# Attention probabilities and output rows turned as fp32 pairs of bf16

## The chip, the cores and the metric

The kernel runs on one core of a Trainium2 chip. The core has a matrix engine (TensorE, PE below, with its weight loads apart), a vector engine (VectorE, DVE), a scalar engine (ScalarE, ACT), GpSimd (POOL), and SyncE (SP), which here only issues DMAs. The metric is the device time of one launch in microseconds, lower is better.

## The reference

Two parts follow each other. A chunked attention: 4 batches, 8 heads, 768 tokens, head size 64. Each chunk of 32 queries sees 8 memory rows and a window of its own chunk with 16 tokens to the left and 8 to the right, so 64 keys.

```python
scores = scale * np.matmul(q_c, k_full.transpose(0, 1, 3, 2))
scores = scores - np.max(scores, axis=-1, keepdims=True)
a = np.exp(scores)
a = a / (np.sum(a, axis=-1, keepdims=True) + 1e-09)
out[:, :, c_start:c_end] = np.matmul(a, v_full)
```

Then a mixture of experts over the 3072 tokens of width 512 that come out: a router with noise picks two of 8 experts for each token, and each expert is a ReLU layer of width 1024.

```python
noisy_logits = logits + noise_scale * noise
top2 = np.argpartition(-noisy_logits, 2, axis=1)[:, :2]
...
h = np.maximum(x[mask] @ w1[e], 0.0)
out[mask] += top2_w[mask, k, None] * (h @ w2[e])
```

## The kernel before

The first stage holds attention and routing, the second the experts. The first runs a loop of 12 steps (`NT`, L538), three for each batch. Step `i` works on two tiles of 128 tokens (`j` = 0, 1) for all 8 heads at once. `b` is the batch, `tp` the step within it.

A step's own work, with the tiles that the prediction names:

- `scores` (L394): PE multiplies queries with keys and memory keys into `ps_s` (two banks of PSUM, one buffer); DVE takes the maximum (L416) and subtracts it (L418) into `sc`.
- `exps` (L421): ACT takes the exponential of the 1024 numbers of each row (L423) into `pb`, in bf16. For each head the two token tiles stand behind one another: 64 numbers of tile 0, 64 of tile 1.
- `turn_p` (L427): for each head PE turns a 128 by 128 block of `pb` against the bf16 identity `identb` (L430), eight turns, and ACT copies the result out of PSUM into `pT` (L433). A block holds both token tiles of one head, so after the turn tile 0 has partitions 0 to 63 and tile 1 has 64 to 127.
- `values` (L436): PE sums the rows with `ones2` (L440), multiplies with the value rows `vb` in 64 small products (L447), DVE takes the reciprocal (L452) and multiplies it in, one instruction for each token tile (L455), into `xrow`.
- `turn_x` (L461): the output rows of the step before are turned in eight blocks (L465) and copied by ACT into `xT` (L467); `gate` (L470) multiplies them with the router's weights `wgn` (L477).
- `keep_x` (L481): the rows go to DRAM, from where the experts gather them.

Beside that each step prepares later ones: `mix` (L349, by POOL after the start) orders loaded rows, `copy_unit` turns them on PE (L366) and copies them into `kT`, `qT` or `vT` (L375, nearly all by ACT), `windows` (L377) turns values into the window rows of `vb` (L383) with a copy by DVE (L386), and `memory_rows` (L388) sends the memory values `mvn` into `vb` by DMA from SP. At the second and third step of a batch a part of the routing of the batch before runs on DVE (L219 to L317).

In this stage the order on PE, ACT, DVE and SP is the order in which the program is written (`manual_schedule`, L512). Turned tiles of all kinds share three PSUM buffers (`psT`). Before the loop, memory keys, memory values and router weights come in through `stage`; the memory values are cast on DVE (L138), the router's weights by L143.

In the second stage `mm1` (L672) and `mm2` (L687) run the experts on tiles of 128 tokens that share the same two experts; the rows come in by gathers of POOL (L638) and leave by scatters (L644).

Of the kernel before, what the change touches and what calls it, by code (L numbers as in the profile page):

```python
# [22 lines left out]
def kernel(  # L23
# [104 lines left out]
    make_identity(nc, identb)  # L128

# [7 lines left out]
    mvn = keep.tile([B * NM, Dm], BF16, name="mvn")  # L137
    nc.vector.tensor_copy(mvn.rearrange("m (c g d) -> m c g d", c=HP, g=2), mvs.rearrange("m (g c) d -> m c g d", g=2))  # L138
    wgs = stage[:, 2 * D + Dm:2 * D + Dm + KP * 2 * E].rearrange("p (k e) -> p k e", k=KP)
    nc.scalar.dma_start(out=wgs[:, :, 0:E], in_=moe_w_gate.rearrange("(kp p) e -> p kp e", p=128))  # L140
    nc.scalar.dma_start(out=wgs[:, :, E:2 * E], in_=moe_w_noise.rearrange("(kp p) e -> p kp e", p=128))
    wgn = const.tile([128, KP, 2 * E], BF16, name="wgn")
    nc.vector.tensor_copy(wgn, wgs)  # L143
# [233 lines left out]
    def windows(b, tp, half):  # L377
        p_v = psT.tile([128, 2, HP, 128], BF16, name="p_v", tag="ps_t")
        for i in range(2):
            c0 = (8 * tp + 2 * half + i) * CH  # L380
            for c in range(HP):
                for j in range(2):
                    nc.tensor.transpose(out=p_v[j * 64:j * 64 + 64, i, c, :],  # L383
                                        in_=vT[:, c, c0 + j * 128:c0 + j * 128 + 64],
                                        identity=identb, tile_position=(0, j * 64))
        nc.vector.tensor_copy(vb[b % 2][:, tp, 2 * half:2 * half + 2], p_v)  # L386

    def memory_rows(b, tp):  # L388
        for j in range(2):
            r0 = j * 64 + WIN  # L390
            nc.sync.dma_start(out=vb[b % 2][r0:r0 + NM, tp].rearrange("m r c w -> m r (c w)"),
                              in_=mvn[b * NM:(b + 1) * NM].unsqueeze(1).to_broadcast([NM, 4, Dm]))

    def scores(t):  # L394
        b, tp = divmod(t, TP)
        q_, k_ = qT[b % 2], kT[b % 2]
        ps_s = psS.tile([128, HP, 2, 2, KW], F32, name="ps_s")
        for j in range(2):
            tk = (2 * tp + j) * 128
            for c in range(HP):  # L400
                nc.tensor.matmul(out=ps_s[:, c, j, :, WIN:KW], lhsT=q_[:, c, tk:tk + 128],
                                 rhs=mkT[:, c, b], start=True, stop=True)
        for j in range(2):
            for c in range(HP):
                for r in range(4):
                    tr = (2 * tp + j) * 128 + r * CH
                    nc.tensor.matmul(out=ps_s[r * CH:(r + 1) * CH, c, j, :, 0:WIN], lhsT=q_[:, c, tr:tr + CH],  # L407
                                     rhs=k_[:, :, c, tr:tr + WIN], start=True, stop=True,
                                     tile_position=(0, r * CH))
        if tp == 0:  # L410
            nc.vector.memset(ps_s[0:CH, :, 0, :, 0:LC], NEG)
        if tp == TP - 1:
            nc.vector.memset(ps_s[128 - CH:128, :, 1, :, WIN - RC:WIN], NEG)
        s3 = ps_s.rearrange("p c j g w -> p (c j g) w")
# [6 lines left out]
    def exps(sc):  # L421
        pb = work.tile([128, H, 2, KW], BF16, name="pb")
        nc.scalar.activation(out=pb.rearrange("p (g c) j w -> p g (c j) w", g=2),  # L423
                             in_=sc.rearrange("p (n g) w -> p g n w", g=2), func=Act.Exp, scale=scale)
        return pb

    def turn_p(pb):  # L427
        p_p = psT.tile([128, H, 128], BF16, name="p_p", tag="ps_t")
        for x in range(H):
            nc.tensor.transpose(out=p_p[:, x, :], in_=pb[:, x].rearrange("p j w -> p (j w)"),  # L430
                                identity=identb)
        pT = work.tile([128, H, 128], BF16, name="pT")
        nc.scalar.copy(pT, p_p)  # L433
        return pT

    def values(t, pT, between=None):  # L436
        b, tp = divmod(t, TP)
        ps_g = psG.tile([128, H, 2], F32, name="ps_g", tag="ps_g")
        for x in range(H):
            nc.tensor.matmul(out=ps_g[:, x], lhsT=pT[:, x, :], rhs=ones2, start=True, stop=True)  # L440
        ps_o = psO.tile([128, 2, H, D], F32, name="ps_o")
        for x in range(H):
            g, c = divmod(x, HP)
            for r in range(4):
                for j in range(2):
                    rows = slice(j * 64, j * 64 + 64)
# [542 lines left out]
```

## Time and profile before

| | us |
|---|---|
| median of 3 runs | 368.08 (367.45 to 370.07) |
| the profiled execution | 364.76 |
| its span, first to last instruction | 363.1 |
| PE busy in the span | 293.6 |
| DVE busy | 178.5 |
| ACT busy | 145.5 |
| POOL busy | 131.7 |

The page gives for each engine the busy time, then the span in 40 slices with the busy share in tenths, then groups of instructions as: line, engine, operation, output and input, shapes, count, busy time and mean of one in ns, and behind the bar the time that the engine sat idle just before them and what ended it. Matmul durations include the way through the array, so that eight in a row take far less than eight times one. "PEld" are the weight loads, which can lie under matmuls. The clock of PE is given as a share of its full speed.

### The profile page before, as it was taken

What the parts mean: (1) busy time and instruction counts of PE and PEld (TensorE: products, weight loads), DVE (VectorE), ACT (ScalarE), POOL (GpSimd) and SP (SyncE); (2) the same over time, 40 slices, a digit from 0 to 9 for tenths busy, and PEclk for the clock granted to TensorE, in tenths of its full rate; (3) what the DMA queues carried; (4) which work ended last, traced back from release to release, by engine and by line L of the source; (5) the groups of instructions that cost most, each with busy time, mean ns of one, the idle gap of its engine ahead of it and who ended that gap; (6) DMA issues with size and microseconds to landing.
All of it is one profiled execution on the core that took longest, in us unless ns stands there. A gap on an engine that the chain in (4) does not pass through costs nothing.

```text
span 363.1 us, 8521 instructions
## 1 busy us (share of the span) xinstructions
PE 293.6 (81%) x3636; PEld 195.0 (54%) x3636; DVE 178.5 (49%) x408; ACT 145.5 (40%) x202; POOL 131.7 (36%) x173
## 2 busy tenths in 40 slices
PE   0577777767776634299999999999999999999990
PEld 0566666656665533185554446666446666555540
DVE  7855565898799787631123410695320134322230
ACT  1446778866853513024433134312244311343400
POOL 6297254554030022572651734063174023201132
PEclk9999798896988755589999999999999999999997
DMA  7999869994949520149799999962059992100012
GB/s 130 213 213 202 160 126 216 210 219 77 201 92 181 127 65 31 33 121 152 126 205 229 202 158 217 152 89 98 23 151 172 193 225 86 54 25 3 23 49 75
DMA packets 44156, 48.33 MB, mean 133 GB/s; under 512 B 19367, under 2 KB 33447, under 8 KB 44112
## 3 DMA queue, kind: packets, MB, share of 16 engines
q0 software_dynamic: 22672, 40.51, 58.8%
q1 hardware_dynamic: 17296, 7.08, 11.4%
q10 hardware_dynamic: 4144, 0.13, 0.8%
q8 instruction: 30, 0.49, 0.5%
q14 instruction: 14, 0.11, 0.1%
HBM read 64.88 MB, written 10.55 MB: 208 GB/s over the span
## 4 chain that ended last, share of the span: by engine, by line
PE 32%; issue 18%; POOL 5%; DVE 4%; DMA 3%; POOLq 1%
PE p_h L681 17%; PE p_y L690 13%; POOL out_dram L644 4%; DMA out_dram<-y,main_dst 1%; DMA xTt<-xt 1%; DMA xt<-xd,main_src 1%; DVE w_all L455 1%; POOL xt L638 1%; DVE oh_l L303 1%; POOL w_all L816 0%; PE p_list L315 0%; PE p_xt L658 0%; POOLq L984 0%; DVE cum L297 0%; PE p_x L465 0%
## 5 line engine op out<-in xcount | busy, mean ns | idle before, releaser
L681 PE MATMUL p_h<-xTt,w_all 128*128 128x256 bf16 (+3 forms) x672 | 101.7, 311 | 0.0
L690 PE MATMUL p_y<-w_all,h 128*128 128x512 bf16 x448 | 100.0, 379 | 0.0
L681 PEld LDWEIGHTS <-w_all 128*128 128x128 bf16 x672 | 65.1, 99 | 34.8 <-issue 0.2
L669 ACT ACTIVATE h<-p_h 128x512 bf16<-128x512 f32 (+1 forms) x79 | 43.5, 551 | 91.2 <-PE p_h L681 80.2
L690 PEld LDWEIGHTS <-h 128*128 128x128 bf16 x448 | 43.7, 98 | 50.0
L667 DVE TENSOR_SCALAR h<-p_h 128x512 bf16<-128x512 f32 (+1 forms) x47 | 29.6, 630 | 75.7 <-PE p_h L681 69.4
L644 POOL DMA_INDIRECT out_dram<-y,main_dst x28 | 31.0, 1108 | 93.8 <-DVE y L696 72.1
L350 POOL COPY w_all<-w_all 128x1024 bf16<-128x1024 bf16 x30 | 30.6, 1044 | 28.9 <-PE p_t L366 27.3
L696 DVE SCALAR_TENSOR_TENSOR y<-p_y,main_w,y 128x512 f32<-128x512 f32 x28 | 21.0, 750 | 39.0 <-PE p_y L690 38.4
L366 PE MATMUL p_t<-identb,w_all 128*128 128x128 bf16 x288 | 27.9, 262 | 11.6 <-DVE w_all L350 7.2
L638 POOL DMA_INDIRECT xt<-xd,main_src x28 | 27.2, 972 | 23.2 <-DMA xTt<-xt 10.4
L694 ACT ACTIVATE y<-p_y,main_w 128x512 f32<-128x512 f32 x28 | 19.3, 689 | 36.5 <-PE p_y L690 35.4
L366 PEld LDWEIGHTS <-w_all 128*128 128x128 bf16 x288 | 23.2, 120 | 13.2 <-DVE w_all L350 7.6
L375 ACT COPY kT<-p_t 64x1024 bf16<-64x1024 bf16 x21 | 21.2, 1008 | 13.6 <-DVE kT L375 10.7
L383 PE MATMUL p_v<-identb,w_all 128*64 128x128 bf16 x384 | 19.0, 256 | 4.8 <-ACT w_all L375 3.3
L308 POOL TENSOR_TENSOR vals<-ohp,facts 128x1008 bf16<-128x1008 bf16 (+2 forms) x5 | 6.6, 1310 | 40.4 <-DVE facts L276 40.4
L433 ACT COPY pT<-p_p 128x1024 bf16<-128x1024 bf16 x12 | 12.1, 1010 | 21.3 <-PE p_p L430 21.1
L383 PEld LDWEIGHTS <-w_all 128*64 128x64 bf16 x384 | 15.1, 132 | 8.2 <-ACT w_all L375 4.2
L455 DVE TENSOR_TENSOR w_all<-ps_o,rs 128x512 bf16<-128x512 f32 x24 | 15.5, 686 | 6.2 <-PE ps_o L447 5.7
L467 ACT COPY xT<-p_x 128x1024 bf16<-128x1024 bf16 x12 | 12.2, 1013 | 13.9 <-PE p_x L465 13.9
L386 DVE COPY w_all<-p_v 128x1024 bf16<-128x1024 bf16 x24 | 16.2, 684 | 2.6 <-PE p_v L383 2.6
L416 DVE TENSOR_REDUCE mx<-ps_s 128x16 f32<-128x1024 f32 x12 | 14.7, 1224 | 4.6 <-PE ps_s L407 4.3
(177 smaller groups left out, 289.6 us busy)
## 6 DMA issues: line engine op xcount, KB each, us to landing
w_all<-in_moe_w_dram POOLq DMA_DIRECT2D x16, 1024.0 KB, 14.2
w_all<-in_moe_w_dram POOLq DMA_DIRECT2D x8, 512.0 KB, 13.9
w_all<-in_k_dram POOLq DMA_DIRECT2D x4, 768.0 KB, 10.4
w_all<-in_q_dram POOLq DMA_DIRECT2D x4, 768.0 KB, 9.6
w_all<-in_v_dram POOLq DMA_DIRECT2D x4, 768.0 KB, 12.1
xd<-w_all SPq DMA_DIRECT2D x12, 256.0 KB
w_all<-mvn SPq DMA_DIRECT2D x24, 32.0 KB
xt<-xd,main_src POOLq DMA_INDIRECT x28, 3.3
```

The source lines that it names most:

```text
L350: i = eng.tensor_copy(home(n, part).rearrange("p s g d -> p g s d"), nat[n % 4].rearrange("p g (s d) -> p g s d", s=SP_)[:, :, part * 8:pa ...
L366: nc.tensor.transpose(out=p_t[:, s, :], in_=m[:, s].rearrange("p g d -> p (g d)"), identity=identb)
L375: (nc.scalar.copy if eng else nc.vector.tensor_copy)(to, src[rows])
L383: nc.tensor.transpose(out=p_v[j * 64:j * 64 + 64, i, c, :], in_=vT[:, c, c0 + j * 128:c0 + j * 128 + 64], identity=identb, tile_position=( ...
L638: i = nc.gpsimd.indirect_dma_start(out=xts[key].bitcast(I32), out_offset=None, in_=xd, in_offset=bass.IndirectOffsetOnAxis(ap=ix, axis=0))
L644: i = nc.gpsimd.indirect_dma_start(out=out if rows is None else rows, out_offset=bass.IndirectOffsetOnAxis(ap=ix, axis=0), in_=y, in_offse ...
L667: nc.vector.tensor_scalar(out=out_, in0=in_, scalar1=0.0, scalar2=None, op0=Alu.max)
L669: nc.scalar.activation(out=out_, in_=in_, func=Act.Relu)
L681: nc.tensor.matmul(out=o, lhsT=w(kp * F + f * 128, 128), rhs=x[:, kp], start=(kp == 0), stop=(kp == KP - 1))
L690: nc.tensor.matmul(out=p, lhsT=h[:, (f * n + j) * 128:(f * n + j + 1) * 128], rhs=w(KP * F + f * Dm, Dm), start=(f == 0), stop=(f == FB - 1))
L694: nc.scalar.activation(out=y, in_=p, func=Act.Copy, scale=weight)
L696: nc.vector.scalar_tensor_tensor(out=y, in0=p, scalar=weight, in1=y, op0=Alu.mult, op1=Alu.add)
```

## The change

Two neighbouring bf16 numbers are read as one fp32 number, and the turn moves them together.

- `pb` keeps the two token tiles next to one another (`[128, H, KW, 2]` for `[128, H, 2, KW]`), so each fp32 number holds the probabilities of tile 0 and tile 1 for the same key. ACT's exponential writes every second bf16. A block of 128 fp32 numbers now holds two heads, so the turned block has the first head of the pair on partitions 0 to 63 and the second on 64 to 127. Four turns do what eight did, and ACT copies 512 fp32 numbers in a row instead of 1024 bf16.
- Hence the value rows stand by parity of the head, not by token tile: `windows` and `memory_rows` put even heads on partitions 0 to 63 and odd ones on 64 to 127, the memory values are kept in two orders (`mvn[:, par]`), the scores are laid out by token tile first, and the value products and sums read every second column of `pT`.
- The output rows are turned in the same way: a number holds two neighbouring columns, the gate reads every second element of `xT`, and the router's weights are loaded in the matching order.
- The identity in fp32 (`identf`) is one more copy on DVE; the memory values are cast by four copies on ACT in place of one on DVE.

The counts and the order of all other instructions on the engines stay as they were.

```diff
+    identf = const.tile([128, 128], F32, name="identf")
+    nc.vector.tensor_copy(identf, identb)
...
-    mvn = keep.tile([B * NM, Dm], BF16, name="mvn")
-    nc.vector.tensor_copy(mvn.rearrange("m (c g d) -> m c g d", c=HP, g=2), mvs.rearrange("m (g c) d -> m c g d", g=2))
...
+    mvn = keep.tile([B * NM, 2, Dm], BF16, name="mvn")
+    for par in range(2):
+        for j in range(2):
+            nc.scalar.copy(mvn[:, par].rearrange("m (c j g d) -> m j c g d", c=2, j=2, g=2)[:, j],
+                           mvs.rearrange("m (g c r) d -> m r c g d", g=2, r=2)[:, par])
...
+    for n, w in enumerate((moe_w_gate, moe_w_noise)):
+        nc.scalar.dma_start(out=wgs[:, n].rearrange("p (k c) -> p k c", k=2), in_=w.rearrange("(k p r) e -> p k (r e)", p=128, r=2))
...
-                    nc.tensor.transpose(out=p_v[j * 64:j * 64 + 64, i, c, :],
+                    nc.tensor.transpose(out=p_v[c % 2 * 64:c % 2 * 64 + 64, i, c // 2, j, :],
...
-        ps_s = psS.tile([128, HP, 2, 2, KW], F32, name="ps_s")
+        ps_s = psS.tile([128, 2, 2, HP, KW], F32, name="ps_s")
...
-        pb = work.tile([128, H, 2, KW], BF16, name="pb")
-        nc.scalar.activation(out=pb.rearrange("p (g c) j w -> p g (c j) w", g=2),
-                             in_=sc.rearrange("p (n g) w -> p g n w", g=2), func=Act.Exp, scale=scale)
+        pb = work.tile([128, H, KW, 2], BF16, name="pb")
+        nc.scalar.activation(out=pb.rearrange("p x w j -> p j x w"),
+                             in_=sc.rearrange("p (j x) w -> p j x w", j=2), func=Act.Exp, scale=scale)
...
-        for x in range(H):
-            nc.tensor.transpose(out=p_p[:, x, :], in_=pb[:, x].rearrange("p j w -> p (j w)"),
-                                identity=identb)
-        pT = work.tile([128, H, 128], BF16, name="pT")
-        nc.scalar.copy(pT, p_p)
+        both = pb.rearrange("p x w j -> p (x w j)").bitcast(F32)
+        for x in range(HP):
+            nc.tensor.transpose(out=p_p[:, x, :], in_=both[:, x * 128:(x + 1) * 128], identity=identf)
+        pT = work.tile([128, HP, 128, 2], BF16, name="pT")
+        nc.scalar.copy(pT.rearrange("p x q j -> p (x q j)").bitcast(F32), p_p.rearrange("p x q -> p (x q)"))
...
-            nc.tensor.matmul(out=ps_g[:, x], lhsT=pT[:, x, :], rhs=ones2, start=True, stop=True)
+                nc.tensor.matmul(out=ps_g[:, j, x], lhsT=pT[:, x, :, j], rhs=ones2, start=True, stop=True)
...
-                                     lhsT=pT[rows, x, r * CH:(r + 1) * CH],
-                                     rhs=vb[b % 2][rows, tp, r, c, g * D:(g + 1) * D],
-                                     start=True, stop=True, tile_position=(j * 64, r * CH))
+                                         lhsT=pT[rows, x, r * CH:(r + 1) * CH, j],
+                                         rhs=vb[b % 2][rows, tp, r, 2 * c + j, g * D:(g + 1) * D],
+                                         start=True, stop=True, tile_position=(par * 64, r * CH))
...
-            for kp in range(KP):
-                nc.tensor.transpose(out=p_x[:, kp, j, :], in_=xr[:, j, kp * 128:(kp + 1) * 128], identity=identb)
-        xT = work.tile([128, KP, 2, 128], BF16, name="xT")
-        nc.scalar.copy(xT, p_x)
+            both = xr[:, j].bitcast(F32)
+            for k in range(2):
+                nc.tensor.transpose(out=p_x[:, j, k, :], in_=both[:, k * 128:(k + 1) * 128], identity=identf)
+        xT = work.tile([128, 2, 2, 128, 2], BF16, name="xT")
+        nc.scalar.copy(xT.rearrange("p j k t r -> p (j k t r)").bitcast(F32), p_x.rearrange("p j k t -> p (j k t)"))
...
-                nc.tensor.matmul(out=ps_l[:, j, :], lhsT=xT[:, kp, j, :], rhs=wgn[:, kp, :],
+                nc.tensor.matmul(out=ps_l[:, j, :], lhsT=xT[:, j, kp // 2, :, kp % 2], rhs=wgn[:, kp, :],
```

62 lines of the change are left out of this document (31 added, 31 removed).

## The prediction

> **What bounds the kernel now.** I read the slices first, then the windows by stage, then one step of the attention loop in order of time, then the groups by line.
>
> ```profile
> span 363.1 us, 8521 instructions
> ...
> PE 293.6 (81%) x3636; PEld 195.0 (54%) x3636; DVE 178.5 (49%) x408; ACT 145.5 (40%) x202; POOL 131.7 (36%) x173
> ...
> PE   0577777767776634299999999999999999999990
> ...
> DVE  7855565898799787631123410695320134322230
> ACT  1446778866853513024433134312244311343400
> ```
>
> A slice is 9.08 us. The first 17 (to about 155 us) are attention and routing; the rest is the expert stage, where TensorE is full. The change touches the first stage alone. What it wins or loses there should reach the end undiminished: the experts' first rows can be gathered only when routing is done, and PE has no slack behind that.
>
> ```profile
> 20.00:40.00 20.00, 15.14 (x346) 13.22 (x344) 10.53 (x14) 13.49 (x14) 15.07 (x17) 0.91 1.13 208
> 40.00:60.00 20.00, 14.10 (x401) 12.60 (x403) 12.26 (x19) 15.33 (x17) 9.10 (x10) 0.88 0.78 151
> 60.00:80.00 20.00, 14.80 (x412) 13.19 (x408) 16.41 (x44) 14.65 (x17) 9.70 (x9) 0.87 1.15 212
> ...
> 100.00:120.00 20.00, 13.52 (x403) 11.91 (x398) 16.99 (x40) 10.07 (x11) 3.52 (x3) 0.83 0.82 146
> 120.00:136.00 16.00, 8.33 (x205) 7.38 (x201) 13.67 (x41) 4.49 (x6) 1.87 (x1) 0.61 0.31 79
> ...
> 163.00:363.00 200.00, 191.56 (x1180) 105.32 (x1178) 60.45 (x120) 61.55 (x107) 64.14 (x65) 0.99 0.68 123
> ```
>
> The columns are the busy time of PE, its weight loads, DVE, ACT and POOL, then granted clock, DMA share and GB/s. ACT leads DVE up to 60 us; from there DVE leads, and past 120 us ACT is nearly idle. So a cut on ACT can pay in the steps before some 65 us, and little behind. One step (i = 2):
>
> ```profile
> 50.72 1.01 ACT L433 COPY pT<-p_p 128x1024 bf16<-128x1024 bf16 x1 [1.33 <-PE p_p L430]
> 51.78 0.61 PE L465 MATMUL p_x<-identb,w_all 128*128 128x128 bf16 x8 [0.59 <-ACT pT L433]
> ...
> 52.42 1.01 ACT L467 COPY xT<-p_x 128x1024 bf16<-128x1024 bf16 x1 [0.69 <-PE p_x L465]
> ...
> 53.33 4.08 ACT L375 COPY kT<-p_t 64x1024 bf16<-64x1024 bf16 x4
> ...
> 57.44 1.06 ACT L423 ACTIVATE pb<-sc 128x1024 bf16<-128x1024 f32 x1
> ...
> 58.55 1.03 PE L430 MATMUL p_p<-identb,pb 128*128 128x128 bf16 x8 [0.70 <-ACT pb L423]
> ...
> 59.67 1.01 ACT L433 COPY pT<-p_p 128x1024 bf16<-128x1024 bf16 x1
> ```
>
> This is a ring: the copy of the turned probabilities, the turn of the output rows, their copy, the copies of keys, the exponential, the turn of the next probabilities, the next copy. It takes 59.67 - 50.72 = 8.95 us, and ACT is busy in all of it but the two turns. Both copies that the change shortens lie on it.
>
> **The two copies.**
>
> ```profile
> L433 ACT COPY pT<-p_p 128x1024 bf16<-128x1024 bf16 x12 | 12.1, 1010 | 21.3 <-PE p_p L430 21.1
> L467 ACT COPY xT<-p_x 128x1024 bf16<-128x1024 bf16 x12 | 12.2, 1013 | 13.9 <-PE p_x L465 13.9
> ```
>
> ```profile
> L669 ACT ACTIVATE h<-p_h 128x512 bf16<-128x512 f32 x40 | 23.9, 598 | 58.5 <-PE p_h L681 53.2 <-DVE dst L914 5.2
> L694 ACT ACTIVATE y<-p_y,main_w 128x512 f32<-128x512 f32 x28 | 19.3, 689 | 36.5 <-PE p_y L690 35.4 <-PE p_xt L757 1.0
> ```
>
> The same bits go over as 512 numbers of four bytes in place of 1024 of two. The trace has no plain fp32 copy of 512 on ACT. The nearest rows are the ReLU out of fp32 PSUM (598 ns) and the scaled one that also writes fp32 (689 ns, but with a scale for each partition, which the copy hasn't). I take 598: 0.41 us less for a copy, 0.32 by the other row. Over 24 copies that is 9.9 us of ACT's time; what counts is how much of it is on a path.
>
> **The turns on PE.** Eight narrow transposes become four wide ones, 96 in place of 192. In the compiled program a wide one is one weight load and one matmul, as a narrow one is. No fp32 operand reaches PE in this trace. Eight narrow ones took 0.61 us (L465 above) and 1.03 us where the clock was low (L430 above). If a wide one costs what a narrow one does, a turn is halved: 0.3 to 0.5 us less. If it passes at a quarter of the rate, four cost as much as sixteen narrow ones: 0.6 to 1.0 us more. I take the price of two narrow ones, so no change: the same bytes at the same rate, between the two ends.
>
> The Trainium skill, "TensorE: Matmul & The Clock Gate", speaks against the halved turn: by its section on weight-path modes the fast weight load is on only where the type is not FP32. By its section on LDWEIGHTS a slow load of 128 columns takes 128/1.2 = 107 ns, so an estimate of 0.43 us for four; its "Terms" add that transpose mode makes FP32 four times faster on trn2, which speaks against the quarter rate. No trace shows either yet; by these figures the turn stays as it is, and the sum below too.
>
> **Strides.** The exponential will write every second bf16, and the row sums, the value product and the gate read their weights in steps of two. No such step is in the trace. Copies into runs with gaps cost ACT nothing: four of L375 take 4.08 us, as dense ones do. The bounds are nothing, and an exponential twice as long, 1.06 us more a step. I take nothing, by L375. DVE's multiply L455 and its other instructions keep their element counts and their order.
>
> **The start.**
>
> ```profile
> 1.48 0.90 POOL L112 DMA_DIRECT2D w_all<-in_k_dram  x1 [0.84 <-POOLq L973]
> ...
> 9.45 0.41 DVE L138 CAST mvn<-w_all 32x512 bf16<-32x512 f32 x1 [0.86 <-DMA w_all<-in_mem_v_dram]
> ...
> 10.01 1.01 DVE L350 COPY w_all<-w_all 128x1024 bf16<-128x1024 bf16 x3
> ...
> 12.91 3.27 ACT L375 COPY kT<-p_t 64x1024 bf16<-64x1024 bf16 x3 [10.69 <-DVE kT L375]
> ```
>
> ```profile
> DMA to landing us min/median/max: 7.2/11.4/15.9
> ```
>
> The cast of the memory values leaves DVE, with its wait of 0.86 us and most of its 0.41. The keys landed at 1.48 + 7.2 = 8.7 us at the earliest, so the next copy on DVE (L350) can go up to 1.1 us sooner; all else of the start waits in line behind it. The fp32 identity comes back onto DVE ahead of the key copies: a copy of 128 numbers, some 0.2 us by the cast's 0.41 for 512. That leaves 0.9 us. The cast becomes four copies on ACT, which has nothing until 12.91: four of at most 0.41 from 9.45 end at 11.1, hidden. If mem_v landed after 11.3, they would push the key copies. The gate weights keep two DMAs; nobody waits for them.
>
> **Which steps let it through.**
>
> ```profile
> 31.21 4.08 ACT L375 COPY kT<-p_t 64x1024 bf16<-64x1024 bf16 x4 [0.69 <-PE p_t L366]
> ```
>
> ```profile
> 46.51 1.01 ACT L375 COPY w_all<-p_t 128x1024 bf16<-128x1024 bf16 x1 [0.40 <-PE p_t L366]
> ```
>
> ```profile
> 91.91 0.26 DVE L452 RECIPROCAL rs<-ps_g 128x16 f32<-128x16 f32 x1 [0.52 <-PE ps_g L440]
> ...
> 96.30 1.22 DVE L418 TENSOR_TENSOR sc<-ps_s,mx 128x1024 f32<-128x1024 f32 x1 [0.45 <-ACT pb L423]
> ```
>
> ```profile
> 65.30:86.10 20.80, 13.65 (x352) 12.16 (x347) 19.36 (x46) 14.82 (x18) 9.21 (x9) 0.83 0.99 184
> 96.30:113.60 17.30, 11.32 (x345) 10.30 (x349) 16.17 (x44) 10.06 (x12) 3.52 (x3) 0.89 0.79 144
> 121.80:135.00 13.20, 5.53 (x140) 4.78 (x137) 12.13 (x36) 4.28 (x6) 1.87 (x1) 0.63 0.21 61
> ```
>
> ```profile
> 119.37 0.67 PE L447 MATMUL ps_o<-w_all,pT 64*32 64x64 bf16 x63 [0.50 <-DMA w_all<-mvn]
> ...
> 120.17 1.29 DVE L455 TENSOR_TENSOR w_all<-ps_o,rs 128x512 bf16<-128x512 f32 x2 [1.86 <-PE ps_o L447]
> ```
>
> Step 0 has one copy, ahead of ACT's long run from 31.21: 0.41. In step 1 ACT waits for PE at 46.51, in a line that runs from the first copy past the second: 0.41. Steps 2 and 3 let both through: 0.82 each. From 65.3 to 86.1 us DVE is busy for 19.36 of 20.80, its own chain: nothing, and likewise from 96.3 to 113.6 and from 121.8 to 135. At 91.91 DVE waits for row sums of the copied probabilities: 0.41. At 96.30 it waits for the exponential behind both copies: most of its 0.45, I take 0.36. Its last long wait, at 120.17, is for a DMA of memory rows, and behind it DVE's own routing sets the end: nothing. Sum: 0.9 + 0.41 + 0.41 + 0.82 + 0.82 + 0.41 + 0.36 = 4.1 us. The profiled execution took 364.76 us (span 363.1), 3.3 under the median of the three runs; it would take 360.7, and the same saving put on the median gives 368.08 - 4.1 = **364.0 us**. Faster or slower by over 1%, about what can be told from no change, means below 364.4 or above 371.8.
>
> **The rivals.** *The copies hide.* Behind ACT's copies stands PE's own row of turns, row sums and value products; step 1 shows it. If it holds steps 2 and 3 as well, each passes 0.41, and if DVE's line at 91.91 is as long, that goes too: 4.1 - 1.2 = 2.9 us, 365.2 us. For it speaks the low clock, 0.88; against it that step 2 has no ACT wait but the turns.
>
> *The wide turn is as slow as sixteen narrow ones.* Some nine turns lie on the path of the sum (both in steps 1 to 3, one or two at 91.91, one at the end); at 0.6 us more each they take 5.4 back: 368.08 + 5.4 - 4.1 = 369.4 us, no change by 1%.
>
> *The wide turn also stops overlapping.* This one ends slower: were the load at a quarter rate as well and ahead of its matmul, a turn would be twice that long again, near 2.5 us for 0.61, so 1.9 us more on nine turns: 368.08 + 17 - 4.1 = 381 us. It decides for slower once a turn grows by (4.1 + 3.7)/9 = 0.9 us. Nothing in the trace tells this from the row above, since it has no wide operand; the single load in the program speaks against.
>
> *The change does not shorten the copies.* If ACT goes by bytes and not by numbers, 512 fp32 cost as much as 1024 bf16; only the start's 0.9 is left: 367.2 us. L669 against L433 speaks against: the time follows the count.
>
> **How the numbers follow.** Forecast 0.52, its own range 361.5 (halved turns on some five places, 2 to 2.5 us more) to 364.6 (0.32 a copy). Copies hidden 0.16, copies not shortened 0.04, quarter rate 0.12, no overlap or strides that cost 0.16. Faster over 1%: 0.50, from the forecast less its upper edge. Within 1%: 0.33. Slower: 0.17. The range that leaves two in ten out goes from 361.0, the forecast's halved turns, to 369.5, the quarter rate; only the last rival is left out and the forecast's far end.
>
> **What would show it.** In the changed profile: L438 and L475 (the two copies) near 0.6 us; four matmuls of a turn no longer than 0.6 us in the middle steps; the first DVE copy of keys at about 8.9 us; ACT below 137 us busy (145.5 now); DVE's first long run without gaps, from 65.3 now, reached 3.4 us sooner. A turn over 1.2 us, or an exponential over 1.5 us, would make the forecast wrong.

## The result, and the profile after

| | before | after |
|---|---|---|
| median of the runs, us | 367.81 (365.63 to 370.46, 13 runs) | 370.05 (368.84 to 374.32, 13 runs) |
| the profiled execution, us | 364.76 | 370.05 |
| its span, us | 363.1 | 368.3 |

The ratio, estimated over all these runs, is 1.007, with a 95% interval of 1.004 to 1.0099: slower by 0.7%, 2.6 us of 367.81 (the two medians are 2.2 us apart). That is within the 1% that the prediction called no change, but it forecast 364.0 us, 4.1 faster, with a range that ended at 369.5. In the ratios of the experiments below, runs more than 1.5% above the fastest of the same kernel are left out, at most four (of thirteen in again2, of twelve in dense).

First the busy times of the changed kernel, then its groups for the two copies and the exponential (line numbers have moved by five to eight: L428 is the exponential, L438 and L475 the copies, L436 and L473 the turns), and last the exponential of the kernel before:

```profile
span 368.3 us, 8328 instructions
...
PE 294.2 (80%) x3520; PEld 193.1 (52%) x3540; DVE 178.5 (48%) x408; ACT 140.3 (38%) x206; POOL 131.6 (36%) x173
```

```profile
L428 ACT ACTIVATE pb<-sc 128x1024 bf16<-128x1024 f32 x12 | 16.2, 1350 | 0.8 <-DVE sc L423 0.7
L475 ACT COPY xT<-p_x 128x512 f32<-128x512 f32 x12 | 7.0, 586 | 16.6 <-PE p_x L473 16.6
L438 ACT COPY pT<-p_p 128x512 f32<-128x512 f32 x12 | 7.0, 585 | 24.2 <-PE p_p L436 24.2
```

```profile
L423 ACT ACTIVATE pb<-sc 128x1024 bf16<-128x1024 f32 x12 | 12.8, 1065 | 0.4 <-DVE sc L418 0.3
```

The copies do what was forecast: 585 and 586 ns for 1010 and 1013, 10.2 us of ACT in 24 copies. But the exponential, which now writes every second bf16, takes 1350 ns in place of 1065: 0.285 us more, 3.4 us in twelve, in the same ring. The four casts of the memory values add 1.3. By the page ACT is 5.2 us less busy, not 9.9.

The step shown before the change (i = 2), in order of time:

```profile
49.26 0.59 ACT L438 COPY pT<-p_p 128x512 f32<-128x512 f32 x1 [1.83 <-PE p_p L436]
50.10 1.12 PE L473 MATMUL p_x<-identf,w_all 128*128 128x128 f32 x4
...
51.25 0.59 ACT L475 COPY xT<-p_x 128x512 f32<-128x512 f32 x1 [1.40 <-PE p_x L473]
...
51.85 4.07 ACT L380 COPY kT<-p_t 64x1024 bf16<-64x1024 bf16 x4
...
55.95 1.33 ACT L428 ACTIVATE pb<-sc 128x1024 bf16<-128x1024 f32 x1
...
57.34 0.66 PE L436 MATMUL p_p<-identf,pb 128*128 128x128 f32 x4 [1.30 <-ACT pb L428]
58.22 0.59 ACT L438 COPY pT<-p_p 128x512 f32<-128x512 f32 x1
```

It takes 58.22 - 49.26 = 8.96 us; it took 8.95. The two copies give 0.84, the exponential takes 0.27 back, and ACT waits 1.40 instead of 0.69 for the output rows, which PE turned in 1.12 us at half clock where it had taken 0.61 at full clock. The next probabilities, turned at full clock this time, give some 0.2 back.

Nor did the steps around it get shorter. The copies of the probabilities of step 0 and of step 4, before, after, and in the kernel that has neither the strided write nor the long wait (dense_pad64, below):

```profile
29.51 1.01 ACT L433 COPY pT<-p_p 128x1024 bf16<-128x1024 bf16 x1 [3.80 <-PE p_p L430]
...
68.00 0.99 ACT L433 COPY pT<-p_p 128x1024 bf16<-128x1024 bf16 x1
```

```profile
27.87 0.59 ACT L438 COPY pT<-p_p 128x512 f32<-128x512 f32 x1 [3.80 <-PE p_p L436]
...
66.85 0.57 ACT L438 COPY pT<-p_p 128x512 f32<-128x512 f32 x1
```

```profile
27.96 0.58 ACT L444 COPY pT<-p_p 128x512 f32<-128x512 f32 x1 [4.10 <-PE p_p L442]
...
63.88 0.57 ACT L444 COPY pT<-p_p 128x512 f32<-128x512 f32 x1
```

From one to the other it is 38.49 us before, 38.98 after and 35.92 in the third; in four further profiles with the changed attention (again, again2, load_late, load_held) it is 38.04 to 39.81. The prediction's sum had 0.41 + 0.41 + 0.82 + 0.82 = 2.5 us won in this stretch.

At step 6 the changed kernel is ahead, by little more than the 1.64 us that it had won by step 0: that step's probabilities are copied at 87.52 us, against 89.58 before. The copies of steps 6 and 7 before, and of step 6 after:

```profile
89.58 1.01 ACT L433 COPY pT<-p_p 128x1024 bf16<-128x1024 bf16 x1 [1.57 <-PE p_p L430]
...
97.50 0.99 ACT L433 COPY pT<-p_p 128x1024 bf16<-128x1024 bf16 x1
```

```profile
87.52 0.59 ACT L438 COPY pT<-p_p 128x512 f32<-128x512 f32 x1
```

Then comes step 7. Its loop body computes the scores of step 8, and so the expectations below call this place step 8:

```profile
92.37 0.53 PE L412 MATMUL ps_s<-kT,qT 128*32 128x112 bf16 x28
93.23 1.34 ACT L428 ACTIVATE pb<-sc 128x1024 bf16<-128x1024 f32 x1
...
95.67 0.23 PE L412 MATMUL ps_s<-kT,qT 128*32 128x112 bf16 x4 [2.78 <-issue]
95.84 1.07 PE L388 MATMUL p_v<-identb,w_all 128*64 128x128 bf16 x16
96.01 0.11 DVE L418 MEMSET ps_s<- 32x64 f32 x1 [3.49 <-PE ps_s L412]
...
96.83 1.12 PE L436 MATMUL p_p<-identf,pb 128*128 128x128 f32 x4
...
97.99 0.59 ACT L438 COPY pT<-p_p 128x512 f32<-128x512 f32 x1 [2.15 <-PE p_p L436]
```

28 of 32 score products run, then PE stands for 2.78 us before the last four and waits for nothing that the profile shows ("issue"). DVE waits 3.49 us for the scores, ACT for the turn queued behind them on PE. The copy at 97.99 is 0.49 us later than before the change: 2.5 us lost in one step. In the windows DMA is full there:

```profile
92.00:94.00 2.00, 0.90 (x41) 1.00 1.16 212
94.00:96.00 2.00, 0.33 (x8) 0.95 1.10 175
```

(stretch, its length, PE's busy time, granted clock, DMA share, GB/s). It is an expert's weights that come in, issued at 86.25 us. The page has a queue of another kind:

```profile
q8 instruction: 29, 0.48, 0.5%
```

29 transfers of 16 KB (transfers, MB, share). One begins at 82.70 us and the next only at 93.40, landing at 94.35, in the middle of PE's wait. That these blocks carry PE's instructions is not written there; the experiments on their place and on the load, below, bear it out.

The two profiled executions differ by 5.2 us, the medians by 2.2. The first product of the experts starts 155.54 - 154.50 = 1.0 us later. The other 4.2 us come behind it, and they are not the change's. The first product and the first ReLU: before, after, and in a kernel with the start alone changed (below):

```profile
154.50 0.42 PE L681 MATMUL p_h<-xTt,w_all 128*128 128x128 bf16 x2
...
157.54 0.60 ACT L669 ACTIVATE h<-p_h 128x512 bf16<-128x512 f32 x1 [4.76 <-PE p_h L681]
```

```profile
155.54 0.42 PE L689 MATMUL p_h<-xTt,w_all 128*128 128x128 bf16 x2
...
160.85 0.60 ACT L677 ACTIVATE h<-p_h 128x512 bf16<-128x512 f32 x1 [7.08 <-PE p_h L689]
```

```profile
153.10 0.42 PE L681 MATMUL p_h<-xTt,w_all 128*128 128x128 bf16 x2
...
157.74 0.60 ACT L669 ACTIVATE h<-p_h 128x512 bf16<-128x512 f32 x1 [6.30 <-PE p_h L681]
```

From the first product to the end of the span is 208.6 us before and 212.8 after. In the profiles below it is 207.7 to 210.2 in all eight of two sets of kernels run together and 211.8 to 213.4 in all ten of the other three sets, kernels with the old attention and the new in both. So it goes with the set (why stays open), and the attention is compared by the start of the experts' first product. Each ratio below is to the kernel before, run on the same chip in the same set.

### The profile page after: what moved, and what is told of

It is laid out like the page before. It is cut to its first block, busy times and chain, and to the rows that moved or that the text cites. A ratio compares the mean times of both kernels' runs of the same rounds, so it can differ in the third digit from the quotient of the medians.

```text
span 368.3 us, 8328 instructions
## 1 busy us (share of the span) xinstructions
PE 294.2 (80%) x3520; PEld 193.1 (52%) x3540; DVE 178.5 (48%) x408; ACT 140.3 (38%) x206; POOL 131.6 (36%) x173
## 4 chain that ended last, share of the span: by engine, by line
issue 23%; PE 20%; POOL 8%; DVE 7%; DMA 2%; another core or an unknown queue 2%; POOLq 1%; DVEq 0%
PE p_y L698 9%; PE p_h L689 9%; POOL out_dram L652 6%; POOL xt L646 2%; DMA out_dram<-y,main_dst 1%; DVE w_all L462 1%; DMA xt<-xd,main_src 1%; DVE oh_l L308 1%; DVE h L675 1%; DVE y L704 0%; PE p_list L320 0%; PE p_xt L666 0%; POOLq L992 0%; DVE cum L302 0%
## 5 line engine op out<-in xcount | busy, mean ns | idle before, releaser
L689 PE MATMUL p_h<-xTt,w_all 128*128 128x256 bf16 (+3 forms) x669 | 103.1, 313 | 1.3 <-issue 1.0
L698 PE MATMUL p_y<-w_all,h 128*128 128x512 bf16 x431 | 98.6, 379 | 2.3 <-ACT y L702 1.4
L689 PEld LDWEIGHTS <-w_all 128*128 128x128 bf16 x672 | 65.8, 101 | 36.8 <-issue 2.1
L371 PE MATMUL p_t<-identb,w_all 128*128 128x128 bf16 x288 | 25.4, 247 | 12.2 <-DVE w_all L355 6.0
L371 PEld LDWEIGHTS <-w_all 128*128 128x128 bf16 x288 | 21.3, 112 | 14.4 <-issue 7.3
L423 DVE TENSOR_TENSOR sc<-ps_s,mx 128x1024 f32<-128x1024 f32 x12 | 14.7, 1225 | 3.8 <-ACT pb L428 2.9
L428 ACT ACTIVATE pb<-sc 128x1024 bf16<-128x1024 f32 x12 | 16.2, 1350 | 0.8 <-DVE sc L423 0.7
L438 ACT COPY pT<-p_p 128x512 f32<-128x512 f32 x12 | 7.0, 585 | 24.2 <-PE p_p L436 24.2
```

Source lines behind the costliest of these rows:

```text
L371: nc.tensor.transpose(out=p_t[:, s, :], in_=m[:, s].rearrange("p g d -> p (g d)"), identity=identb)
L689: nc.tensor.matmul(out=o, lhsT=w(kp * F + f * 128, 128), rhs=x[:, kp], start=(kp == 0), stop=(kp == KP - 1))
L698: nc.tensor.matmul(out=p, lhsT=h[:, (f * n + j) * 128:(f * n + j + 1) * 128], rhs=w(KP * F + f * Dm, Dm), start=(f == 0), stop=(f == FB - 1))
```

## The experiments

Three theories. 1: the exponential's strided write takes the copies' gain back. 2: blocks of TensorE's instructions come late; the change took 16 instructions out of each step, so that another product stands at the end of a block. 3: PE's own row in the ring, at a lower granted clock, hides what ACT saves.

| kernel | ratio (95%) | experts' first product, us | PE's waits "issue" over 0.4 us in the attention, us |
|---|---|---|---|
| changed, again | 1.0077 (1.0045 to 1.0109) | 154.70 | 1.63, **2.66** |
| changed, again2 | 1.0035 (1.0007 to 1.0062) | 158.96 | 2.19, 1.89, **3.42** |
| dense | 1.0006 (0.9972 to 1.0039) | 155.06 | 1.07, **3.02** |
| sc_pairs | 1.0042 (1.0002 to 1.0081) | 158.33 | 2.15, 1.37, **3.92** |
| start | 0.9989 (0.9958 to 1.0019) | 153.10 | 1.50, 0.52 |
| after_pad32 | 1.0034 (1.0006 to 1.0063) | 155.02 | 1.35 |
| after_pad64 | 1.0014 (0.9983 to 1.0045) | 153.10 | 0.62, 1.08, 0.74 |
| pad64_again | 0.9993 (0.9965 to 1.0022) | 153.60 | 0.47, 0.92 |
| after_pad96 | 1.0044 (1.0013 to 1.0074) | 152.75 | 1.55, 2.65, 0.97 |
| after_pad128 | 1.0081 (1.0051 to 1.0112) | 154.91 | 1.18, **3.44** |
| before_pad64 | 1.0063 (1.002 to 1.0106) | 154.78 | 0.97, 0.91, 2.52, 0.47 |
| load_late | 1.0089 (1.0054 to 1.0124) | 157.09 | 1.23, **3.30** |
| load_held | 0.9984 (0.9946 to 1.0022) | 150.23 | 1.42 |
| dense_pad64 | 0.9974 (0.9944 to 1.0003) | 150.62 | 0.82, 0.88, 1.43 |
| sc_pairs_pad64 | 0.9967 (0.9935 to 0.9998) | 153.53 | 1.53, 2.31 |
| x_only_pad28 | 0.9961 (0.9927 to 0.9995) | 154.33 | 1.34 |
| p_only_pad32 | 0.9998 (0.9969 to 1.0028) | 153.25 | 1.73 |
| x_start_pad28 | 0.995 (0.9921 to 0.9978) | 151.53 | 1.97 |

Bold is the wait before the last four score products. The third column is of one profile each: the changed program's own four profiles (155.54 above, again, again2, load_late) lie between 154.70 and 158.96 us. Nor is a ratio surer than its interval: again2 and load_late are the same program in the same set, and stand at 1.0035 and 1.0089. An effect of half a per cent needs more than one measurement.

**The changed kernel again**, three times: again, again2 and, as it came out, load_late.

> The changed kernel once more, unaltered, for a second profile of it. If the wait of TensorE's sequencer of 2.78 us at 92.9 us (four score products of step 8 that wait for nothing that the profile shows) belongs to this program, it stands in this profile too, between 91 and 97 us, with 2 to 3.5 us; if it belonged to that one execution, it is under 1 us or stands elsewhere. The same for the first relu of the expert stage, which ScalarE began 5.3 us after the stage's first product (3.0 us before the change). The time should again be 1.004 to 1.010 of the kernel before.

> The changed kernel unaltered, beside the three that follow on the same chip: 1.004 to 1.010 of the kernel before, and again a wait of 2.5 to 3.9 us at the last four score products of step 8.

The long wait stands in every profile, at the same four products, so it is the program's. The late first ReLU is not: 5.31 us after the first product in the first profile, 3.85 and 3.16 in these two.

**The strided write.** The first kernel takes it away and leaves the counts; the second moves it to VectorE, with the reference's output.

```diff
-        nc.scalar.activation(out=pb.rearrange("p x w j -> p j x w"),
-                             in_=sc.rearrange("p (j x) w -> p j x w", j=2), func=Act.Exp, scale=scale)
+        nc.scalar.activation(out=pb.rearrange("p x w j -> p (x w j)"),
+                             in_=sc.rearrange("p n w -> p (n w)"), func=Act.Exp, scale=scale)
```

```diff
-        sc = work.tile([128, 2 * H, KW], F32, name="sc", bufs=1)
-        nc.vector.tensor_tensor(out=sc, in0=s3, in1=bc(mx, KW), op=Alu.subtract)
+        sc = work.tile([128, H, KW, 2], F32, name="sc", bufs=1)
+        nc.vector.tensor_tensor(out=sc.rearrange("p x w j -> p j x w"), in0=s3.rearrange("p (j x) w -> p j x w", j=2),
+                                in1=bc(mx, KW).rearrange("p (j x) w -> p j x w", j=2), op=Alu.subtract)
...
+        nc.scalar.activation(out=pb, in_=sc, func=Act.Exp, scale=scale)
```

> The changed kernel with the exponential written in the order in which it is computed (the probabilities then stand before the wrong value rows, so the attention's values are not the reference's; all counts and sizes are kept). Theory 1, the strided write: the exponential falls from 1350 to about 1065 ns, twelve times, 3.4 us of ScalarE, of which the eight to ten steps in which ScalarE or the chain through it sets the pace carry 2.3 to 2.9 us: 367.2 to 367.8 us against 370.05, that is within 0.3% of the kernel before. Theory 2, TensorE's wait of 2.78 us at 92.9 us and the slower start of the expert stage: they stay, and the time falls by less than 1 us (369.1 to 370.1). Theory 3, TensorE's own row of work in the shortened ring (its granted clock 0.79 instead of 0.88 in the second and third step): what ScalarE saves is waited for at TensorE, the time falls by less than 1 us.

> The changed kernel with the two neighbours put side by side by VectorE: the subtraction of the maximum writes its fp32 result at every second place, and the exponential reads and writes in order; the output is the reference's. If the subtraction keeps its 1225 ns and the exponential falls to about 1065 ns, this is worth the same as the dense exponential, 2.3 to 2.9 us by theory 1 and under 1 us by theories 2 and 3. If VectorE pays for the strided write as ScalarE did (a quarter more, 0.3 us each), the gain is smaller by what of VectorE's row is in the ring (it is in four steps at most): 1.5 to 2.5 us by theory 1.

The groups by line: the exponential of the first, the exponential of the second, and the subtraction of the second (its view by source line: count, ns as minimum, median and maximum).

```profile
L428 ACT ACTIVATE pb<-sc 128x1024 bf16<-128x1024 f32 x12 | 12.7, 1062 | 0.8 <-DVE sc L423 0.7
```

```profile
L429 ACT ACTIVATE pb<-sc 128x1024 bf16<-128x1024 f32 x12 | 12.7, 1061 | 0.9 <-DVE sc L423 0.9
```

```profile
L423 DVE TENSOR_TENSOR sc<-ps_s,mx x12: 1224/1225/1227, 21.3 to 126.9; 128x1024 f32<-128x1024 f32 x12
```

So the write alone makes the 0.29 us, and VectorE's subtraction takes no longer (1225 ns) when it writes fp32 at every second place. In time, the dense one is 0.7% below the changed kernel of its set, clear of it by both intervals; the one in pairs 0.35%, not clear. The mean of the two, 1.0024, against that of the four measurements of the changed program (1.0070, 1.0077, 1.0035, 1.0089), 1.0068, is 0.44%; with 64 idle products added (below) it is 0.33% (0.9971 against 1.0004). That makes some 1.2 to 1.6 us of the 3.4. The dense kernel keeps its long wait of 3.02 us: neither theory alone holds.

**The place of the blocks.** At the start, where PE is idle, small products that nobody reads; two instructions each.

```diff
+    p_pad = psT.tile([128, 64], F32, name="p_pad", tag="ps_t")
+    for x in range(64):
+        r = x % 4
+        nc.tensor.matmul(out=p_pad[r * CH:(r + 1) * CH], lhsT=identb[:, r * CH:(r + 1) * CH], rhs=identb[:, 0:64],
+                         start=True, stop=True, tile_position=(0, r * CH))
```

> The changed kernel with 64 small products of the identity (128 instructions of TensorE, 0.7 to 2 us of its idle time at 5.6 to 9.1 us, read by nobody). The change took 16 instructions of TensorE out of each step, so that a block of 256 instructions ends elsewhere; the padding puts about what was taken up to step 8 back. Theory 2, late instructions: the wait of 2.7 to 3.9 us at 92 to 98 us, which ended 1.2 to 1.5 us after a block of instructions had landed in every profile of this program, goes or falls under 1 us, VectorE's maximum of step 8 no longer waits for it, and the time falls by 1.5 to 2.8 us to about 366.5 to 367.8 (beside a kernel before at 366.7). Theory 1, the strided write alone: a wait may move, but the time stays at 1.005 to 1.009 of the kernel before.

> The changed kernel with 64 products of the identity once more, on the same chip as the one before it: again no wait of over 1.2 us of TensorE's sequencer in the attention, and 0.998 to 1.004 of the kernel before.

> The same with 32 products (64 instructions). Theory 2: the blocks end another quarter of a block elsewhere, so the waits for instructions stand at other places in the attention, and the time moves with the sum of those that stop ScalarE's ring: between 0.5 us above and 2.8 us below the changed kernel, in step with the waits over 0.5 us in its own profile. Theory 1: the time stays at 1.005 to 1.009 of the kernel before, whatever the waits.

> The same with 96 products (192 instructions). Theory 2 and theory 1 as for 32 products: by theory 2 the three paddings differ from one another by 1 to 3 us, in the order of the waits for instructions in their profiles; by theory 1 all three are within 0.5 us of the changed kernel.

> The changed kernel with 128 products of the identity at the start: 256 instructions, a whole block, so that the blocks end at the same places in the attention as without padding. If the place of the blocks decides (late instructions), the long wait is back at the last four score products of step 8 with 2.5 to 3.9 us, and the time is that of the changed kernel, 1.004 to 1.010. If the padding helped in another way (a warmer clock at the start, another order of buffers), the time stays near that of 64 products, 0.999 to 1.003, without the long wait.

> The kernel before with the same 64 products at the start. Theory 2: the waits of 1.6 us at 54.9 and 0.6 us at 68.0 us move too, and where one comes to stand in a step that TensorE or ScalarE bounds, the time grows by 1 to 3 us (368 to 370); if the padding only removes them, it falls by up to 1 us. Theory 1: no change, within 0.5 us of the kernel before.

The same place with 64 products (L418 is the score product there), in order of time:

```profile
92.33 0.58 PE L418 MATMUL ps_s<-kT,qT 128*32 128x112 bf16 x32
92.83 0.64 PE L394 MATMUL p_v<-identb,w_all 128*64 128x128 bf16 x16
94.55 0.66 PE L442 MATMUL p_p<-identf,pb 128*128 128x128 f32 x4 [1.08 <-ACT pb L434]
```

All 32 products run, and the turn follows at full clock, 2.3 us sooner than at 96.83 in the changed kernel. With 128 products, a block of 256 instructions further, the wait is back at the same four products (3.44 us) and the time with it (1.0081). So for this wait it is the place of the blocks, and no warming or order of buffers. And the kernel before, given 64 products, gets such a wait of its own:

```profile
94.54 0.58 PE L389 MATMUL p_v<-identb,w_all 128*64 128x128 bf16 x13
97.64 0.30 PE L389 MATMUL p_v<-identb,w_all 128*64 128x128 bf16 x3 [2.52 <-issue]
```

It is then at 1.0063: without any change of what it computes, as slow as the changed kernel. What failed is the order among 32, 64 and 96: by the waits in their profiles 96 should have been the slowest by far, but its interval overlaps those of the others and its profile reaches the experts at 152.75 us. So the length of the waits alone does not give the time; that it depends on which step they fall into is likely, but not shown. Nor does taking the long wait away always win as much: it is gone with 32 and 96 products too, and their 1.0034 and 1.0044 are only 0.3 and 0.2% below the changed program's mean of 1.0068, where 64 products, in two measurements, are 0.5 and 0.75% below it.

**The load.** The first kernel writes the issue of the third expert's weights one step later; the second makes GpSimd wait with it for logits.

```diff
-            if i in (3, 4, 6):
-                load_expert({3: 0, 4: 1, 6: 2}[i])
+            if i in (3, 4, 7):
+                load_expert({3: 0, 4: 1, 7: 2}[i])
```

```diff
+            if i == 7:
+                held = work.tile([128, 1], F32, name="held")
+                pin(nc.gpsimd.tensor_copy(held, lgs[(i - 1) // TP][:, 2 * ((i - 1) % TP), 0:1]))
+                load_expert(2)
```

> The changed kernel with the load of the third expert (2 MB, issued at 86.3 us, its packets fill the transfer engines until about 100 us) issued one step later, at about 95 us; nothing else is altered, TensorE's instructions are the same. If the block of instructions that lands at 93.4 us is late because it queues behind that load, it lands by 90 us, the wait at the last four score products of step 8 falls under 0.7 us, and the time falls by 1 to 2.8 us (0.999 to 1.004) unless a later block meets the load in its new place. If the block is late for a reason of its own, the wait stays at 2.5 us or more.

> The changed kernel with the third expert's load held on GpSimd by a copy of one logit per row of step 7, which VectorE writes at about 92.5 us: the load is issued at about 92.7 instead of 86.3 us. TensorE's instructions are the same. If the block of instructions that lands at 93.4 us queues behind this load's packets, it lands at 87 to 91 us, the wait at the last four score products of step 8 falls under 0.7 us, and this step's probabilities are copied 2 us or more sooner than in the changed kernel; the time falls to 0.999 to 1.004 unless the next block (99.8 us) is held up by the load in its new place, which would then show a wait of 1 us or more between 97 and 106 us. If the block is late for a reason of its own, the wait of 2.5 us or more stays where it is.

The first came out as the same program: GpSimd has nothing between the two places, and issued the load at 86.48 us as ever. It counts as a further run of the changed kernel and tells nothing of the load. The second held the load until 99.68, not 92.7 as expected, since the logits are written later in the step than I had read. PE's score products and the copy on GpSimd in its profile:

```profile
89.47 0.78 PE L412 MATMUL ps_s<-kT,qT 128*32 128x112 bf16 x32
```

```profile
99.56 0.19 POOL L596 COPY held<-lg 128x1 f32<-128x1 f32 x1 [16.16 <-DVE d L276]
99.68 0.80 POOL L76 DMA_DIRECT2D w_all<-in_moe_w_dram  x1
```

With TensorE's program unaltered the wait is gone. When the 16 KB block begins to come in, and when PE's wait for it ends, in us, for the changed program and those that share its blocks:

```
kernel         block begins   wait ends   wait
after              93.40        95.67     2.78
again              91.97        94.25     2.66
again2             96.75        99.18     3.42
dense              92.85        95.29     3.02
sc_pairs           96.26        98.69     3.92
after_pad128       92.93        95.12     3.44
load_late          94.82        97.13     3.30
load_held          87.65          -        0
```

The wait ends 2.2 to 2.4 us after the block begins, each time. The block begins 5.8 to 6.8 us after step 6's probabilities are copied in the first seven, and 3.0 us after (84.62) where no load is ahead of it. So the load ahead of it is what makes the block late, by one profile with the load held. The ratio falls to 0.9984 (0.9946 to 1.0022). The experts' first product starts at 150.23 us, 4.3 us sooner than in the kernel before, while the time of many runs cannot be told from that kernel's; what the profile gains in excess of that was not followed further.

**The parts.** The wide turn for the output rows alone, for the probabilities alone, the cast on ScalarE alone, and combinations, with padding for the instructions taken out up to step 8. The one-line start:

```diff
-    nc.vector.tensor_copy(mvn.rearrange("m (c g d) -> m c g d", c=HP, g=2), mvs.rearrange("m (g c) d -> m c g d", g=2))
+    nc.scalar.copy(mvn.rearrange("m (c g d) -> m c g d", c=HP, g=2), mvs.rearrange("m (g c) d -> m c g d", g=2))
```

For the output rows alone `turn_x`, the gate's line and the order of `wgn` are taken from the changed kernel (with `identf`) and all else from the kernel before; for the probabilities alone it is the other way round.

> The kernel before with one part of the change alone: the cast of the memory's value rows is done by ScalarE instead of VectorE at the start. The first copy of the keys should begin 0.9 to 1.15 us sooner, and the first step's scores with it. If what is gained at the start reaches the end, the time is 0.9 to 1.15 us below the kernel before (0.997 of it); if the loads or a wait of TensorE's sequencer take it back, the ratio is 1.000.

> The kernel before with the output rows alone turned as fp32 pairs (their copy 586 instead of 1013 ns, twelve times; the gate's weights rearranged; exponential, values and start as before), with 28 products of the identity for the instructions that this takes away up to step 8. No strided write is left in it. If the shorter copy counts in the steps in which ScalarE's row is full, it is worth 0.43 us in each of four of them: 0.995 to 0.996. If it hides behind TensorE's turn and windows in those steps: 0.999 to 1.001.

> The changed kernel with the output rows turned singly as before: probabilities as fp32 pairs, value rows by parity, the strided exponential and the cast of the memory's rows on ScalarE remain; 32 products of the identity stand for the instructions taken away up to step 8. By the strided write's price of 0.285 us against 0.425 us that the shorter copy saves, each step nets 0.14 us of ScalarE, and the start gives 1.1 us: 0.996 to 0.998. If the strided write costs more than the copy saves (it stands between the scores and the turn, where nobody else works; the copy stands behind the windows): 1.000 to 1.004.

> The output rows alone as fp32 pairs, and the cast of the memory's rows on ScalarE at the start, with 28 products of the identity: the parts of the change that put nothing on the exponential. If both count they add: 0.992 to 0.994 of the kernel before; if the copy hides and the start counts: 0.996 to 0.998; if neither: 0.999 to 1.001.

The output rows alone bring 0.39% (1.4 us; interval 0.05 to 0.73%), with the start 0.5% (1.8 us; 0.22 to 0.79%). The start alone brings 0.11% and cannot be told from nothing, though its profile reaches the experts 1.4 us sooner. This speaks against theory 3, by which the shorter copy hides, but does not settle it: in the profile of the output rows alone the stretch from step 0's copy to step 4's is no shorter (38.68 us, 38.49 before), the experts start only 0.2 us sooner, and the padding puts the instruction blocks back only roughly, a rival that by itself moved the kernel before by 0.6%. The probabilities with the start bring nothing, which fits a strided write that takes back what their copy saves. The version with output rows and start is faster than both kernels by its interval, and has the lowest ratio of all.

**Both causes away.**

> The changed kernel with both suspected costs taken away: VectorE writes the neighbours side by side, so that the exponential takes about 1062 ns, and 64 products of the identity at the start put the blocks of instructions where the long wait at 92 us did not stand. If the strided write and the late instructions are two causes that add, this is their two effects below the changed kernel: the dense exponential's 0.7% and the padding's 0.6% from 1.007, that is 0.993 to 0.996 of the kernel before. If they share a cover (what one saves is waited for in the other's place), it stays at 0.999 to 1.002. If TensorE's own row in the ring holds the time whatever ScalarE does, it is not below the padded kernel with the strided write, 1.0014.

> The changed kernel with the exponential written in the order in which it is computed (the probabilities stand before the wrong value rows) and 64 products of the identity. If the two costs add: 0.7% and 0.6% below the changed kernel's 1.007, 0.992 to 0.996. If the write by VectorE in pairs has a price that its duration of 1225 ns doesn't show, this is 0.3% or more below the kernel that had both, 0.9967; if not, the same within 0.2%.

0.9967 and 0.9974 agree, so the write in pairs has no hidden price, and both stand about 1% below the changed kernel's 1.0068. The effects found one by one, 0.44 and 0.64%, make 1.1%: the two costs add, though 0.992 to 0.996 was expected.

## Why the prediction was wrong, point by point

- *The two copies*: right in size. 598 ns was forecast, 585 measured. That they count on the path is likely by the output rows alone, 1.4 us (0.2 to 2.7), but not sure, as said there.
- *The turns*: right. Four wide ones took 0.66 us at full clock and 1.12 at half clock, eight narrow ones 0.61 and 1.03. The Trainium skill, "TensorE: Matmul & The Clock Gate", section on LDWEIGHTS, gives 128/1.2 ns for 128 columns, so the estimate was 107 ns a load and 0.43 us for four; the trace agrees, with 0.42 us for four wide loads in a row at full clock. A narrow load goes at about twice the pace, eight in 0.45 us (the turns' weight loads, after and before):

```profile
86.64 0.42 PEld L436 LDWEIGHTS p_p<-identf,pb 128*128 128x128 f32 x4 [0.42 <-ACT pb L428]
```

```profile
66.82 0.45 PEld L430 LDWEIGHTS <-pb 128*128 128x128 bf16 x8 [1.36 <-ACT pb L423]
```

  Neither the rival of the quarter rate nor that of no overlap came about.
- *Strides*: the first step that failed. For PE's weight loads in steps of two nothing was right (the row sums' load L446 102 ns against 101, the gate's L485 102 against 100). For the exponential I took nothing "by L375". That row's gaps lie between runs of eight elements; a step of two at every element is another thing, and costs 0.285 us each, a quarter of the upper bound of 1.06. Paid on the path: 1.2 to 1.6 us, by the runs with the write in order. That strides could cost stood among the chances, but with no time of its own.
- *Which steps let it through*: the second step that failed, and the larger, in two places. In steps 0 to 3 the sum counted 2.5 us, and the stretch they make up got no shorter (38.49 us before, 38.04 to 39.81 in five profiles with the changed attention). Four exponentials at 0.285 account for 1.1 us of that. The rest is open: PE's own row at a lower clock, as in the rival that the copies hide, would fit, but with the long wait and the strided write both away one profile has the stretch at 35.92 us, 2.6 shorter. Behind that the sum let the gains at 91.91 and 96.30 pass on to the end, and gave the removed instructions no price but that of the turn. What it left out is that they also move the ends of the instruction blocks. One block now comes behind an expert's load, and its wait of 2.7 to 3.9 us stands just where those gains were counted. Without it the kernel is 0.64% or 2.4 us faster with 64 products (mean 1.0004), and 0.84% or 3.1 us with the load held; with 32 and 96 products, where other waits stand, only 1.2 and 0.9 us. No rival held this. It could have been read: the page lists the instruction queue, and before the change PE already waits so, in time order:

```profile
56.47 0.31 PE L401 MATMUL ps_s<-mkT,qT 128*128 128x16 bf16 x6 [1.61 <-issue]
```

- *The start*: right in the profile (the first copy of keys at 8.72 us for 8.9 forecast, with the fp32 identity's 0.21 us behind it and not ahead; ACT's first at 11.76 for 12.91, 1.15 us sooner), but in the runs of the start alone the gain is 0.4 us, between 1.5 faster and 0.7 slower.
- *Sum*: 4.1 us faster forecast, 2.6 slower measured. Instructions 2.4 to 3.1 (by 64 products and the load held) and the exponential 1.2 to 1.6 make 3.6 to 4.7 of these 6.7 us at best. With both away, 0.9971 is 1.1 us faster, so 2 to 3 us of the forecast stay unexplained. Two things bear on it, neither settled: the padded kernels keep waits of 0.8 to 2.3 us at other places, and step 2 waited 0.71 us more for a turn at half clock. From 40 to 80 us the granted clock was 0.87 in the kernel before and two relatives, but 0.74 to 0.88 in those with wide turns; whether the change causes that was not tried.
- *The signs named*: the copies came as said, the turns near it (0.66 us at full clock, for no longer than 0.6, and up to 1.12 in the middle steps where the clock was low), ACT was busy 140.3 us instead of below 137, DVE's long run without gaps began at 64.44 us, 0.87 sooner and not 3.4, and the exponential at 1350 ns stayed under the 1.5 us that was to make the forecast wrong. That sign was set too high: 0.285 us more in each step undid a third of the sum.

## What to carry to other kernels

When an edit removes instructions from an engine that runs a long unrolled program, its later instruction blocks end elsewhere; look for "issue" waits where DMA is full, before and after, and test with a few idle products ahead, or with the load moved, before the edit is judged. A gain of half a per cent can be smaller than this shift, which here moved an otherwise unaltered kernel by 0.6%, and smaller than the difference between two measurements of one program. Price a strided write at the engine that makes it, and where two engines stand in a row, let the one that pays nothing for the step do it.

## What the runs showed of the hardware

- An exponential of 1024 numbers that writes bf16 at every second place takes 1350 ns, in order 1062; VectorE's fp32 subtraction took 1225 either way. The Trainium skill, "SBUF — State Buffer", section "Door 1: The DMA port swizzle", states that accesses to bf16 can stride by up to eight elements for free; ScalarE's write at a step of two here does not agree.
- PE's instructions come in during the run by blocks of 16 KB, and the load of an expert's weights can hold them up. Behind 2 MB of weights a block began 5.8 to 6.8 us after the copy of step 6, without the load 3.0 us after; PE then stood for 2.7 to 3.9 us, and went on 2.2 to 2.4 us after the block began to come in. 64 idle products, 128 instructions, moved the wait away, and 128 products, 256 instructions, brought it back to the same place.
- Moving a DMA in the program's text moves nothing if its engine has no work between the two places: the same load was issued at 86.25 and 86.48 us.
